# Row maxima of the first unit placed by transposes, and a shorter lead of the max products

## The chip, the cores and the metric

The kernel runs on one core of a Trainium2 chip. The metric is the device time of one execution in microseconds (us). The engines are TensorE (PE, with its weight loads PEld), VectorE (DVE), ScalarE (ACT), GpSimd (POOL) and SyncE (SP), which issues most of the DMA transfers.

## The reference

One block of a transformer with adaptive layer norms, on 2048 rows of 512 numbers in float32:

```python
mod = silu(c) @ w_mod                       # six rows of 512: sa, ca, ga, sb, cb, gb
h = layernorm(x) * (1 + ca) + sa
q = h @ wq                                  # 32 heads of 16
k = h @ wk; v = h @ wv                      # one head of keys and values, shared by all
p = softmax(q @ k.T * 16 ** -0.5)           # 2048 x 2048 for each head
x = x + ga * ((p @ v) @ wo)
h = layernorm(x) * (1 + cb) + sb
x = x + gb * (gelu(h @ w1 + b1) @ w2 + b2)  # 1376 hidden numbers
```

## The kernel before

**Precision.** A float32 number is kept as a high part, rounded to the format fp32r, and the remainder. A product of two such numbers is three products (`mm3`, and `batches` in the loop). The helper `split` makes the two parts; the engines that do it are its arguments.

**Units.** The 2048 rows are cut into 8 blocks of 256, the 32 heads into 8 groups of 4. A block and a group are one unit: 64 units. The queries of a unit lie in a tile `qst` of 128 partitions: its two halves `s` (partitions 0 to 63 and 64 to 127) hold two heads each. The keys lie in `ks` in the same two halves, for all 2048 keys. There are four `qst` tiles, used in turn (`QBUFS`), and `load_q` fills one with six transfers from HBM (eight from the fifth unit on).

**Two passes over the keys.** Softmax needs the largest score of each row. A first pass finds it: 32 *max products* `m` per unit (`Max.step`, L507), each with a reduction on VectorE (L512) that writes one column of `mx`. When the last one of a unit is done, `put_max` is called: VectorE reduces `mx` to 8 columns (L560) and transposes blocks of 32 x 32 (L561); `gather` puts the pieces into 8 rows on GpSimd (L555) and splits them into high part and remainder; `send` issues four transfers (L550) that write them into rows 48, 49, 112 and 113 of `qst`. In `ks` these rows are -1, so the second pass gets scores with the maximum subtracted: products `e` (`sexp`, L612), exponentials `p` on ScalarE (L616), and the products `acc` with the values and a block of ones (`pv`, L633), which sum up numerator and denominator. `finish_unit` copies them out.

**The loop** runs over the units and, in each, over 8 key steps of 256 keys, two at a time: a *pair*. A pair has 8 products `e`, 8 exponentials, 32 products `acc`, 8 max products of units that come later, and possibly one *batch* of weight products (query projections, output projection, the two layers of the network), cut in two halves of the array and mixed in. Weight products come from a queue of generators (`qproj_late`, `rest_steps`). In this loop the order on each engine is the order in which the program emits; it is not rearranged.

**The lead.** `lead[u]` says how many max products have been issued when unit u starts: all of units 0 to u and `4 * LEAD` more. It is 24 more here, so a unit's maxima are complete after the first pair of the unit before it. When no max products are left, the pairs run without them (`alone`).

**The clock.** `clock[0]` counts four ticks a pair. `later(n, fn)` runs `fn` n ticks on. In the loop `put_max` runs `reduce` at the next tick that is 1 above a multiple of four, `gather` `MAX_WAIT[0]` = 1 tick behind that and `send` `MAX_WAIT[1]` = 4 ticks behind it. Units 8 and 9 run `reduce` at once. The layer norm of the second half runs in the same clock: `stats`, `rstd` (L846, L847, L849), `xhat` (L852, GpSimd), `add_bias`, then transposes `tp` (L917, issued in batches).

**The prologue** makes layer norms, keys, values and the first query projections, and places the max products of the first units between them. `SLOTS` writes that order out: a number of max products, then named steps ("q 1": three products of the query projection of group 1, "rows": four vector-matrix products of `late_rows` (`modl`), "v 2": the values of block 2, "wq 2": a weight piece split on ScalarE and GpSimd, "load": `load_q` of unit 2). `FIRST_MAX` gives the order of the max products of units 0 and 1. In the prologue `later` runs its function at once. After the slots, `chunk(1)` goes on until `lead[0]`, 56 max products; `mod_state["rows"]` is copied by ScalarE (L1307, `modl_sb`), and `keep_warm(WARM[3])` issues five products whose result nobody reads (L287).

`ebank` gives out three PSUM banks in turn; the bank "x" holds in turn the key projection of block 3, the rows `modl` and late projections; max products have three banks "m" and in some pairs "x".

Of the kernel before, what the change touches and what calls it, by code (L numbers as in the profile page):

```python
# [8 lines left out]
F32 = mybir.dt.float32  # L9
F32R = mybir.dt.float32r  # L10
AF = mybir.ActivationFunctionType
ALU = mybir.AluOpType
AX = mybir.AxisListType

P = 128
# [3 lines left out]

GELU_R = 0.044715 ** 0.5  # L20

LEAD = 6
LEAD_0 = 6
FIRST_MAX = ((0, 0), (1, 0), (0, 1), (1, 1), (0, 2), (0, 3), (1, 2), (1, 3))
SLOTS = ((2, "keys 1", "keys 1"), (2, "keys 1", "keys 1"), (2, "low 1", "heads 2"), (2, "heads 2", "k 1"), (1, "warm"), (1, "heads 2"), (2, "heads 2", "v 0"),
# [4 lines left out]
MAX_WAIT = (1, 4)  # L30
QBUFS = 4
PREP = 4
BUSY = 5
# [3 lines left out]
TAIL = (4, 8)  # L37
GROUP = 4
NORM_WAIT = 6
WARM = (4, 16, 2, 5)  # L40
MOD_WAIT = 3
AHEAD = 4.5
STIR = ((0, 4, 8, 12), (16, 32, 48, 0))
# [2 lines left out]
def raw(ap):  # L46
    return ap.bitcast(F32)
# [3 lines left out]
def adaln_mqa_mlp(  # L51
# [15 lines left out]
    nc = tc.nc  # L67
    _, S, D = x.shape
# [4 lines left out]
    BQ = 512  # L73
# [4 lines left out]
    NKC = S // 512  # L78
# [28 lines left out]
    ident = const.tile([P, P], F32, name="ident")  # L107
# [16 lines left out]
    def ebank():  # L124
        turns[0] += 1
        return dict(tag=f"e{turns[0] % 3}", bufs=1)

    def split(dst_h, dst_l, src, eng_h, eng_l, between=None):
        if eng_h is nc.gpsimd:
            eng_h.tensor_scalar(out=dst_h, in0=src, scalar1=1.0, scalar2=0.0, op0=ALU.mult, op1=ALU.add)  # L130
        elif eng_h is nc.scalar:
            eng_h.copy(dst_h, src)
        else:
            eng_h.tensor_copy(out=dst_h, in_=src)
        if between:
            between()
        eng_l.tensor_tensor(out=dst_l, in0=src, in1=raw(dst_h), op=ALU.subtract)  # L137
# [7 lines left out]
    def later(n, fn):  # L145
        if draining[0]:
            fn()
        else:
            pending.append((clock[0] + n, fn))
# [7 lines left out]
    def mm3(ps, pairs, every=0, cost=0, begin=True, end=True):  # L157

        n, last = 0, 3 * len(pairs) - 1
        for wh, wl, xh, xl in pairs:  # L160
            for a, b_ in ((wh, xh), (wl, xh), (wh, xl)):
                nc.tensor.matmul(ps, a, b_, start=begin and n == 0, stop=end and n == last)  # L162
                n += 1
                if every and n % every == 0:
                    yield cost
# [48 lines left out]
    pro = pro_ctx.enter_context(tc.tile_pool(name="pro", bufs=1))  # L214
# [210 lines left out]
    def qpairs(b, g):  # L425
        hH, hL = hts[b]
        gs = slice(g * P, (g + 1) * P)
        return [(wqH[:, k, gs], wqL[:, k, gs], hH[:, k, :], hL[:, k, :]) for k in range(KD)]

    def qtiles(b, g):  # L430
        qH = att.tile([P, BQ], F32R, name=f"qH{b}_{g}", tag="xH", bufs=2)
        qL = att.tile([P, BQ], F32R, name=f"qL{b}_{g}", tag="xL", bufs=2)
        return qH, qL

    def qproj(b, g):

        ps = psum.tile([P, BQ], F32, name=f"qps{b}_{g}", tag="v" if g else "x")
        yield from mm3(ps, qpairs(b, g), 3, 1)
        qH, qL = qtiles(b, g)
        if g == 0:  # L440
            nc.scalar.copy(qH, ps)
            nc.vector.tensor_tensor(out=qL, in0=ps, in1=raw(qH), op=ALU.subtract)
        else:
            q32 = pro.tile([P, BQ], F32, name=f"q32_{b}_{g}", tag="h32", bufs=4)
            nc.scalar.copy(q32, ps)
            split(qH, qL, q32, act, pool)
        send_q(b, g, qH, qL)
        yield -2

# [16 lines left out]
    qsts = {}  # L466
# [15 lines left out]
    class Max:  # L482


        def __init__(self):
            def products(u, kcs):
                return [(u, j, t, kc) for kc in kcs for j in range(2) for t in range(blocks[units[u][0]][1] // P)]

            def in_rows(u):
                return [(u, j, t, kc) for j in range(2) for t in range(blocks[units[u][0]][1] // P) for kc in range(NKC)]  # L490


            begin = [o for u, kc in FIRST_MAX for o in products(u, [kc])]
            self.todo = [begin + [o for u in range(2, NU) for o in in_rows(u)] for _ in range(2)]
            self.mx, self.left, self.done = {}, list(size), 0

# [28 lines left out]
    placed = set()  # L525
# [5 lines left out]
    def put_max(u, mx):  # L531

        T = blocks[units[u][0]][1] // P
        qst = qsts[u]
        mm = mms[u % 2]
        turned = att.tile([P, 32], F32, name=f"turned{u}", tag="turned", bufs=2)
        if u == 0:
            pad(att, 256, "pad7")  # L540
        mt = att.tile([4 * T, P], F32, name=f"mt{u}", tag="mt", bufs=2)
        mh = att.tile([4 * T, P], F32R, name=f"mh{u}", tag="mh", bufs=2)
        ml = att.tile([4 * T, P], F32R, name=f"ml{u}", tag="ml", bufs=2)

        def send():
            for s in range(2):
                for r, src in ((48, mh), (49, ml)):
                    dst = qst[64 * s + r:64 * s + r + 1].rearrange("p j (t n) -> p (j t) n", n=P)
                    ring = nc.scalar if u == 0 and s else nc.sync
                    ring.dma_start(out=raw(dst), in_=raw(src[2 * T * s:2 * T * (s + 1), :].unsqueeze(1)))  # L550
            placed.add(u)

        def gather():
            for g in range(0, P, 32):
                nc.gpsimd.tensor_scalar(out=mt[:, g:g + 32], in0=turned[g:g + 4 * T, :], scalar1=1.0, scalar2=0.0,  # L555
                                        op0=ALU.mult, op1=ALU.add)
            split(mh, ml, mt, nc.gpsimd, nc.gpsimd)

        def reduce():
            nc.vector.tensor_reduce(out=mm[:, :4 * T], in_=mx, axis=AX.X, op=ALU.max)  # L560
            nc.vector.transpose(out=turned, in_=mm)  # L561
            later(MAX_WAIT[0], gather)
            later(MAX_WAIT[1], send)


        if NQ <= u < NQ + 2:
            reduce()
        else:
            later((0 - clock[0]) % 4 + 1, reduce)

    pbufs = {}
    ocs = []
# [606 lines left out]
    first = [sum(size[:u]) for u in range(NU + 1)]  # L1179
# [6 lines left out]
    act, dve, pool = nc.scalar, nc.vector, nc.gpsimd  # L1186
# [7 lines left out]
    projections = [qproj(b, g) for b in range(2) for g in range(KD)]  # L1194
# [36 lines left out]
    def q_group():  # L1231
        for i in range(KD):
            next(projections[0])
            if i == KD - 1:
                next(projections.pop(0))
            yield

    def warm():
        keep_warm(WARM[2], tag="x")
        yield  # L1240

    def one(fn, *args):
        fn(*args)
        yield
# [13 lines left out]
    turn1(0, 3)  # L1258
    keep_warm(WARM[0])
    mod1(0, 1, pool, dve, lambda: stats1(1))  # L1260
# [3 lines left out]
    rows = xhat1(1, act)  # L1264
# [17 lines left out]
    def last_h(t):  # L1282
        if t == QT - 1:
# [6 lines left out]
    run(xhat1(3, pool))  # L1290
    keep_warm(WARM[1])
    work = {"keys 1": keys(1), "heads 2": heads(2), "heads 3": heads(3), "q 1": q_group(), "keys 2": keys(2), "keys 3": keys(3),
            "v 0": one(v_out, 0), "v 1": one(v_out, 1), "v 2": one(v_out, 2), "v 3": one(v_out, 3), "rows": late_rows(),
            "low 1": one(low_k, 1), "low 2": one(low_k, 2), "low 3": one(low_k, 3), "k 1": one(repeat_k, 1), "k 2": one(repeat_k, 2), "k 3": one(repeat_k, 3), "load": one(load_q, 2), "warm": warm(),
            "wq 1": one(prep_wq, 1), "wq 2": one(prep_wq, 2), "wq 3": one(prep_wq, 3)}
    for n, *names in SLOTS:
        chunk(n)
# [173 lines left out]
    last = queue.pop()[1]  # L1471
# [49 lines left out]
```

## Time and profile before

| | |
|---|---|
| median of 3 runs | 1561.97 us (1561.87 to 1562.56) |
| profiled execution | 1561.89 us |
| its span, first to last instruction | 1560.1 us |
| prologue, until the first product `e` | 74.95 us |
| max products and their reductions | 2048, VectorE 1269.3 us busy |
| last max product's step ends | 1471.1 us |
| granted TensorE clock | 1.000 |

The profile is of one execution. "Busy" counts the time an engine works on instructions; matmuls overlap, so their durations are longer than their distances. The chain of waits is followed back from the last instruction: at each step to what released it, or to the instruction before it on its engine. In its rows the columns are start, duration, engine and line. In rows of the timeline they are start, duration, engine, line, operation, what is written and read, and in brackets the idle time before and what ended it.

### The profile page before, as it was taken

To read this page: it belongs to the slowest core of one execution; us is meant where nothing else is said; L and a number is where in the kernel's file an instruction comes from. 1 tells how busy PE (TensorE), PEld (TensorE's weight loads), DVE (VectorE), ACT (ScalarE), POOL (GpSimd) and SP (SyncE) were. 2 spreads that over 40 slices of the span, in tenths; PEclk is the share of its full clock that TensorE was granted. 3 is DMA by queue.
4 is the path that set the end of the run, shared out by engine and by line. 5 is a ranking of instruction groups with operands and counts; after the bars stand their busy time and mean duration, and the time that the engine had idled before them with its cause. 6 is when DMAs were issued, how large, how long until landed. Compare 5 with 4: busy or idle time off the path is not lost.

```text
span 1560.1 us, 41350 instructions
## 1 busy us (share of the span) xinstructions
PE 1543.2 (99%) x16347; PEld 955.2 (61%) x16347; DVE 1400.8 (90%) x2479; ACT 1227.4 (79%) x2392; POOL 681.5 (44%) x1194
## 2 busy tenths in 40 slices
PE   7999999999999999999999999999999999999999
PEld 4456555567655665557655675556655676556657
DVE  7999999999999999999999999999999999999725
ACT  5577778788878887788877887788877888778953
POOL 5545433867322570246522562245611474225721
PEclk9999999999999999999999999999999999999999
DMA  7225412312030211202012120302112120211241
GB/s 250 92 93 197 148 56 85 124 52 97 19 109 19 83 59 36 94 28 99 30 54 76 55 86 23 109 14 100 44 49 80 46 97 17 84 55 63 84 159 52
DMA packets 83125, 121.61 MB, mean 78 GB/s; under 512 B 19614, under 2 KB 56222, under 8 KB 82676
## 3 DMA queue, kind: packets, MB, share of 16 engines
q1 hardware_dynamic: 82916, 118.97, 22.9%
q8 instruction: 129, 2.11, 0.6%
q14 instruction: 64, 0.52, 0.1%
q10 hardware_dynamic: 16, 0.00, 0.0%
HBM read 91.13 MB, written 27.27 MB: 76 GB/s over the span
## 4 chain that ended last, share of the span: by engine, by line
PE 84%; DVE 10%; issue 3%; POOL 2%; DMA 1%; ACT 1%; SPq 0%; POOLq 0%; DVEq 0%
PE acc L633 28%; PE m L507 24%; PE e L612 15%; DVE mx L512 8%; PE w1ps L193 8%; PE w2ps L183 2%; PE w1ps L183 1%; DMA xt<-in_A_x_dram 1%; PE w2ps L193 1%; PE qps L193 1%; PE tp L193 1%; PE wops L193 1%; PE kps L162 1%; DVE st L840 1%; DVE x L833 1%
## 5 line engine op out<-in xcount | busy, mean ns | idle before, releaser
L512 DVE TENSOR_REDUCE mx<-m 128x1 f32<-128x512 f32 x2048 | 1269.3, 681 | 87.7 <-PE m L507 64.7
L616 ACT ACTIVATE p<-e 128x512 f32<-128x512 f32 x2048 | 1098.0, 598 | 254.8 <-PE e L612 106.4
L507 PE MATMUL m<-ks,qst 64*128 64x512 f32 x2048 | 832.9, 429 | 2.0 <-DVE mx L512 0.6
L612 PE MATMUL e<-qst,ks 64*128 64x512 f32 x2048 | 739.9, 413 | 0.0
L633 PE MATMUL acc<-p,va 128*32 128x256 f32 x8192 | 548.0, 385 | 0.0
L507 PEld LDWEIGHTS m<-ks,qst 64*128 64x128 f32 x2048 | 367.1, 184 | 211.6 <-DVE mx L512 174.0
L612 PEld LDWEIGHTS e<-qst,ks 64*128 64x128 f32 x2048 | 358.7, 185 | 92.3 <-ACT p L616 64.0
L633 PEld LDWEIGHTS acc<-p,va 128*32 128x32 f32 x8192 | 214.5, 109 | 213.7 <-issue 110.7
L555 POOL TENSOR_SCALAR mt<-turned 8x32 f32<-8x32 f32 x256 | 53.1, 208 | 419.5 <-DVE turned L561 407.4
L193 PE MATMUL w1ps<-h2H,w1t 64*128 64x256 f32 x1216 | 232.7, 287 | 0.0
L193 PEld LDWEIGHTS w1ps<-h2H,w1t 64*128 64x128 f32 x1216 | 183.6, 185 | 28.4 <-issue 14.4
L193 PE MATMUL w1ps<-h2L,w1t 64*128 64x256 f32 x608 | 167.0, 275 | 0.0
L193 PE MATMUL w2ps<-w2H,gH 64*128 64x512 f32 x264 | 115.9, 439 | 0.0
L193 PEld LDWEIGHTS w1ps<-h2L,w1t 64*128 64x128 f32 x608 | 112.8, 185 | 0.0
L193 PE MATMUL w2ps<-w2L,gH 64*128 64x512 f32 x264 | 103.4, 392 | 0.0
L193 PE MATMUL w2ps<-w2H,gL 64*128 64x512 f32 x264 | 103.0, 390 | 0.0
L959 POOL TENSOR_SCALAR tt<-tt 128x256 f32<-128x256 f32 x77 | 31.0, 403 | 143.1 <-ACT tt L958 109.8
L137 POOL TENSOR_TENSOR gL<-z,gH 128x256 fp32r<-128x256 f32 x77 | 56.9, 739 | 6.4
L960 POOL TENSOR_TENSOR tt<-tt,z 128x256 f32<-128x256 f32 x77 | 56.8, 738 | 6.4
L970 POOL TENSOR_TENSOR z<-tt,z 128x256 f32<-128x256 f32 x77 | 56.4, 733 | 6.0
L969 POOL TENSOR_TENSOR tt<-tt,z 128x256 f32<-128x256 f32 x77 | 56.5, 734 | 0.0
L193 PE MATMUL wops<-woH,onH 64*128 64x512 f32 x112 | 49.8, 444 | 0.0
(190 smaller groups left out, 1495.3 us busy)
## 6 DMA issues: line engine op xcount, KB each, us to landing
w1t<-dw SPq DMA_DIRECT2D x82, 512.0 KB
qst<-dq SPq DMA_DIRECT2D x384, 32.0 KB
do<-oc SPq DMA_DIRECT2D x64, 128.0 KB
dw<-w1s SPq DMA_DIRECT2D x11, 512.0 KB
xt<-in_A_x_dram SPq DMA_DIRECT2D x4, 1024.0 KB
dq<-qH SPq DMA_DIRECT2D x16, 256.0 KB
dq<-qL SPq DMA_DIRECT2D x16, 256.0 KB
x<-in_A_x_dram SPq DMA_DIRECT2D x8, 512.0 KB
```

Of the source, the lines that this page charges most:

```text
L137: eng_l.tensor_tensor(out=dst_l, in0=src, in1=raw(dst_h), op=ALU.subtract)
L183: nc.tensor.matmul(ps, a, b_, start=first_, stop=last_)
L193: ins = nc.tensor.matmul(ps, a[rows], b_[rows], start=first_ and s == 0, stop=last_ and s == 1)
L507: nc.tensor.matmul(m, qsts[u][rows, j, t * P:(t + 1) * P], ks[rows, kc * 512:(kc + 1) * 512], start=True, stop=True)
L512: nc.vector.tensor_reduce(out=self.mx[u][:, i, kc:kc + 1], in_=m, axis=AX.X, op=ALU.max)
L555: nc.gpsimd.tensor_scalar(out=mt[:, g:g + 32], in0=turned[g:g + 4 * T, :], scalar1=1.0, scalar2=0.0, op0=ALU.mult, op1=ALU.add)
L612: nc.tensor.matmul(e, ks[rows, kt * P:(kt + 1) * P], rhs, start=True, stop=True)
L616: ins = nc.scalar.activation(dst, e, AF.Exp, scale=0.25)
L633: ins = nc.tensor.matmul(accs[u][32 * cidx:32 * cidx + 32, :], va[:, kt, :], rhs, start=kt == 0, stop=kt == NKT - 1)
L960: nc.gpsimd.tensor_tensor(out=tt, in0=tt, in1=z, op=ALU.mult)
L969: nc.gpsimd.tensor_tensor(out=tt, in0=tt, in1=z, op=ALU.mult)
L970: nc.gpsimd.tensor_tensor(out=z, in0=tt, in1=z, op=ALU.add)
```

## The change

Three things change together.

*The first unit's rows.* For unit 0 `put_max` no longer transposes, gathers and sends. VectorE reduces to 8 columns as before, copies them into column 48 (and, for the second half, 112) of four zeroed 128 x 128 tiles `spots`, and writes the remainder into column 49 (113). A new step, `first_rows`, transposes the four tiles on TensorE into one PSUM bank and adds that bank to the whole `qst` on VectorE. Its rows are thus placed without a transfer. `spots` is cleared by GpSimd in a step of its own.

*The order.* Unit 0's max products are complete after 46 products instead of 48, because one group of unit 1's moves behind them. `LEAD` goes from 6 to 4: the lead is 16 products, the loop starts after 48 instead of 56, and a unit's maxima are complete after the second pair of the unit before it. The slots are rewritten; the query projection's last step becomes a fifth slot, with the remainder on GpSimd and the two transfers there. The five keep-warm products go.

*The waits.* For later units `gather` is called right behind `reduce`, and `send` 2 ticks behind it.

```diff
-LEAD = 6
-LEAD_0 = 6
-FIRST_MAX = ((0, 0), (1, 0), (0, 1), (1, 1), (0, 2), (0, 3), (1, 2), (1, 3))
+LEAD = 4
+LEAD_0 = 4
+FIRST_MAX = ((0, 0, 4), (1, 0, 4), (0, 1, 4), (1, 1, 3), (0, 2, 4), (0, 3, 4), (1, 1, 1), (1, 2, 4), (1, 3, 4))
...
-         (0, "v 2"), (2, "q 1"), (2, "q 1"), (2, "q 1"),
-         (2, "q 1", "rows"), (2, "v 3", "wq 2"), (2, "rows"), (2, "rows"), (2, "rows", "wq 3", "load"))
-MAX_WAIT = (1, 4)
+         (0, "v 2", "q 1", "spots"), (2, "rows"), (2, "q 1"), (2, "q 1", "wq 2"), (2, "q 1"), (2, "q 1", "rows"),
+         (2, "first", "rows", "v 3", "rows", "wq 3", "load"))
+MAX_WAIT = 2
...
-WARM = (4, 16, 2, 5)
+WARM = (4, 16, 2, 0)
...
-            split(qH, qL, q32, act, pool)
+            nc.scalar.copy(qH, q32)
+            yield -2
+            nc.gpsimd.tensor_tensor(out=qL, in0=q32, in1=raw(qH), op=ALU.subtract)
...
+        if u == 0:
+            nc.vector.tensor_reduce(out=mm[:, :4 * T], in_=mx, axis=AX.X, op=ALU.max)
+            src = mm[:, :4 * T].rearrange("p (s n) -> p s n", s=2)
+            dst = spots.rearrange("p n (s c) -> p s n c", s=2)
+            nc.vector.tensor_copy(out=dst[:, :, :, 48], in_=src)
+            nc.vector.tensor_tensor(out=dst[:, :, :, 49], in0=src, in1=raw(dst[:, :, :, 48]), op=ALU.subtract)
+            return
...
-                    ring = nc.scalar if u == 0 and s else nc.sync
-                    ring.dma_start(out=raw(dst), in_=raw(src[2 * T * s:2 * T * (s + 1), :].unsqueeze(1)))
+                    nc.sync.dma_start(out=raw(dst), in_=raw(src[2 * T * s:2 * T * (s + 1), :].unsqueeze(1)))
...
-            later(MAX_WAIT[0], gather)
-            later(MAX_WAIT[1], send)
+            gather()
+            later(MAX_WAIT, send)
...
+    spots = pro.tile([P, 4, P], F32R, name="spots")
+
+    def clear():
+        nc.gpsimd.memset(raw(spots), 0.0)
+
+    def first_rows():
+
+        qst = qsts[0].rearrange("p j n -> p (j n)")
+        ps = psum.tile([P, BQ], F32, name="rows0", **ebank())
+        for n in range(4):
+            nc.tensor.transpose(ps[:, n * P:(n + 1) * P], raw(spots[:, n, :]), ident)
+        nc.vector.tensor_tensor(out=qst, in0=ps, in1=raw(qst), op=ALU.add)
+        placed.add(0)
```

The lines left out are the lists that give the maxima's order one product at a time, the generator of the query projection with its fifth step, the 256-byte padding tile that is now made with unit 1, and the two new names in the table of steps.

More of the change, by code (lines that the diff above doesn't have):

```diff
@@ L490, in in_rows @@
                 return [(u, j, t, kc) for j in range(2) for t in range(blocks[units[u][0]][1] // P) for kc in range(NKC)]
-            begin = [o for u, kc in FIRST_MAX for o in products(u, [kc])]
+            parts = {(u, kc): products(u, [kc]) for u in range(2) for kc in range(NKC)}
+            begin = [parts[u, kc].pop(0) for u, kc, n in FIRST_MAX for _ in range(n)]
+            assert not any(parts.values())
             self.todo = [begin + [o for u in range(2, NU) for o in in_rows(u)] for _ in range(2)]
@@ L537, in put_max @@
         mm = mms[u % 2]
+        if u == 0:
[5 more added lines that the diff above has]
+            return
         turned = att.tile([P, 32], F32, name=f"turned{u}", tag="turned", bufs=2)
-        if u == 0:
+        if u == 1:
             pad(att, 256, "pad7")
@@ L1234, in q_group @@
             if i == KD - 1:
-                next(projections.pop(0))
+                last = projections.pop(0)
+                next(last)
             yield
+        next(last, None)
+        yield
     def warm():
@@ L1293, in adaln_mqa_mlp @@
             "v 0": one(v_out, 0), "v 1": one(v_out, 1), "v 2": one(v_out, 2), "v 3": one(v_out, 3), "rows": late_rows(),
-            "low 1": one(low_k, 1), "low 2": one(low_k, 2), "low 3": one(low_k, 3), "k 1": one(repeat_k, 1), "k 2": one(repeat_k, 2), "k 3": one(repeat_k, 3), "load": one(load_q, 2), "warm": warm(),
+            "low 1": one(low_k, 1), "low 2": one(low_k, 2), "low 3": one(low_k, 3), "k 1": one(repeat_k, 1), "k 2": one(repeat_k, 2), "k 3": one(repeat_k, 3), "load": one(load_q, 2), "warm": warm(), "first": one(first_rows), "spots": one(clear),
             "wq 1": one(prep_wq, 1), "wq 2": one(prep_wq, 2), "wq 3": one(prep_wq, 3)}
```

## The prediction

> **What bounds the kernel now.** I read the page first, then the chain of waits around the first unit, in the steady loop and at its end, then single engines in the windows that the chain names.
>
> ```profile
> PE 1543.2 (99%) x16347; PEld 955.2 (61%) x16347; DVE 1400.8 (90%) x2479; ACT 1227.4 (79%) x2392; POOL 681.5 (44%) x1194
> ...
> PE 84%; DVE 10%; issue 3%; POOL 2%; DMA 1%; ACT 1%; SPq 0%; POOLq 0%; DVEq 0%
> ```
>
> TensorE (PE) is the bound, with VectorE (DVE) close behind: 84% and 10% of the chain. So I price an instruction by whether PE or DVE runs without a pause where it stands. Every key step (K step) ends in 16 products `acc` of 1.00 us, so the distance of these rows is the price of a step. The chain at the end of the loop:
>
> ```profile
> 1468.33 1.00 PE acc L633 x16
> ...
> 1471.17 1.00 PE acc L633 x16
> ...
> 1476.36 1.00 PE acc L633 x16
> ```
>
> With max products a step takes 2.84 us, a pair of steps 5.68. From 1471.17 the max products are used up, and a pair takes 5.19.
>
> The start of the loop, in the same view:
>
> ```profile
> 64.52 0.90 PE qps L162 x3
> 65.42 1.00 PE modl L292 x8
> 66.42 0.43 PE m L507 x2
> ...
> 73.66 0.33 PE idle L287
> 73.99 1.12 issue
> 75.10 0.59 ACT modl_sb L1307
> ```
>
> Here the bound isn't the rows of maxima alone: ScalarE (ACT) copies `modl_sb` at 75.10, when the five keep-warm products have just ended, and every exponential is queued behind that copy. It ends at 75.69.
>
> **The start, step by step.** Up to the value projection of block 2 both kernels issue the same on PE; it starts at 58.42:
>
> ```profile
> 58.42 0.43 PE L414 MATMUL vps<-ident,vt 32*128 32x32 f32 x4
> ```
>
> From there PE runs, in the new order: `vps` (0.36 until the next row), the first q group's three products (0.90), two max products (0.43): 60.1. Now `rows` needs the bank "x", which frees when VectorE has subtracted block 3's keys:
>
> ```profile
> 59.90 0.68 DVE L402 TENSOR_TENSOR ks<-kps,ks 16x512 fp32r<-16x512 f32 x1
> ```
>
> That is 60.6. Then `rows` 1.0, three times max pair and q group (3 x 1.33), the pair that completes unit 0: it starts at 65.6.
>
> ```profile
> 66.89 2.48 DVE L512 TENSOR_REDUCE mx<-m 128x1 f32<-128x512 f32 x4 [1.05 <-PE m L507]
> 69.40 0.19 DVE L560 TENSOR_REDUCE mm<-mx 128x8 f32<-128x32 f32 x1
> ```
>
> A pair's reductions start 0.47 after it (66.42 to 66.89) and take 1.24 (half of 2.48): 67.3. VectorE's three small steps (maxima of maxima, copy into `spots`, remainder) follow. Only the first has a row, 0.19. The other two, 8 numbers a partition, lie between that and the 0.68 of a 512-wide operation; I take 0.2 each, as the row of that size says: 67.9. Meanwhile PE has done the next `rows` and max pair by 67.5 and waits half a microsecond. Behind the waiting transposes stand two `rows`, a `vps` and the loop's first products. The four transposes cost what four of the same size do:
>
> ```profile
> 37.18 0.59 PE tp L375 x4
> ```
>
> They end at 68.6; two `rows` and a `vps` (2.36) end at 70.9. The wide addition on VectorE (0.68, behind two reductions) is done by 70.1 and hidden under them; without that cover it would cost its 0.68. The copy `modl_sb` has no keep-warm products to wait for, and ends 0.6 later: 71.5, with 0.2 for semaphores 71.7. Against 75.69 the loop starts **3.9 us** earlier. With 0.68 for both small steps it is 3.0; with no semaphore cost 4.1. What goes away besides (gather, four row transfers, eight max products) was beside this path or is in it already. What moves with it: the q group's two transfers and `load_q`'s six wait one slot longer, but unit 2's first max product comes 16 products into the loop, two pairs or 11.4 us; GpSimd clears `spots` in a slot in which nothing else is queued on it, ten max products ahead of the first use.
>
> The five keep-warm products go and transposes come, so the clock is to be looked at. This stretch now:
>
> ```profile
> 58.40:75.00 16.60, 15.99 (x81) 6.72 (x79) 14.92 (x26) 5.03 (x12) 5.59 (x12) 1.00 0.10 35
> ```
>
> The granted clock is 1.00, with a pause of 1.12 us in it. I expect it to stay, since the new pauses are of half a microsecond. The Trainium skill, "TensorE: Matmul & The Clock Gate", speaks against this part: PE's clock halves after an idle window of about 3.4 us, and transposes don't count as busy (Part 1 and Part 4). By its window two pauses of half a microsecond cost nothing, by its transposes the margin shrinks; the trace agrees so far that short pauses leave the clock alone. A clock that falls is the last rival.
>
> **The end: one pair more with max products.** The lead shrinks by 8 products, one pair's worth, so the max products last one pair longer. That pair costs 5.68 in place of 5.19: **+0.5**.
>
> **The middle: the reductions move by one pair.** Each later unit's maxima are complete one pair later, so its small reduction and transpose on VectorE move from the unit's second pair to its third. (The program counts four ticks a pair.) In steps that PE bounds this costs nothing: four reductions take 2.35 (the row below has four) of 2.84, and a pair leaves twice the rest, about 1.0, for 0.5. But once per block, seven times,
>
> ```profile
> POOL ve L847 <- DVE mv L846: 27.1, 7, 4.5
> ```
>
> the third pair has no weight products, and VectorE bounds it, loaded with the layer norm's statistics. The chain there:
>
> ```profile
> 852.26 0.24 DVE mv L846 x2
> 852.51 2.35 DVE mx L512 x4
> 854.87 0.04 issue
> 854.91 0.50 PE m L507
> ```
>
> VectorE runs without a pause, and PE's max product at 854.91 waits for it. What is put in front of 852.26 delays it in full. The price, and what the old place gives back:
>
> ```profile
> 845.70 0.17 DVE L560 TENSOR_REDUCE mm<-mx 128x8 f32<-128x32 f32 x1
> 845.98 0.21 DVE L561 STREAM_TRANSPOSE turned<-mm 128x32 f32<-128x32 f32 x1
> ```
>
> ```profile
> 845.60 0.49 PE L507 MATMUL m<-ks,qst 64*128 64x512 f32 x1
> ```
>
> The two take 0.38 us of work and 0.49 from start to end, I use 0.46. At the old place VectorE would only wait for this product, which ends at 846.09, as long as for the two: almost nothing comes back. 7 x 0.46 = **+3.2**. The lower end is zero, if the next steps take it up.
>
> GpSimd (POOL) has the same collision, because the gather now comes at once, in front of `ve` and the two `xh`:
>
> ```profile
> 846.28 1.02 POOL L555 TENSOR_SCALAR mt<-turned 8x32 f32<-8x32 f32 x4 [20.87 <-DVE turned L561]
> 847.38 0.29 POOL L130 TENSOR_SCALAR mh<-mt 8x128 fp32r<-8x128 f32 x1
> 847.75 0.46 POOL L137 TENSOR_TENSOR ml<-mt,mh 8x128 fp32r<-8x128 f32 x1
> 852.60 0.24 POOL L847 TENSOR_SCALAR ve<-mv 128x2 f32<-128x2 f32 x1 [4.39 <-DVE mv L846]
> 852.92 0.72 POOL L849 TENSOR_TENSOR rs<-ve,mhalf 128x2 f32<-128x2 f32 x1
> 853.75 4.15 POOL L852 TENSOR_SCALAR xh<-x,mv,rs 128x512 f32<-128x512 f32 x2
> ```
>
> The gather and split take 1.93 (846.28 to 848.21) and would end near 854.7, so `ve` starts 2.1 later and the second `xh` ends at 860.0 in place of 857.9. The first weight load that needs it:
>
> ```profile
> 859.62 0.30 PEld L193 LDWEIGHTS tp<-ident,xh 64*128 64x128 f32 x2
> ```
>
> It is itself late by the 0.46, 860.08: covered, by almost nothing. Without VectorE's delay, PE would wait 0.4 here instead; the two overlap and don't add.
>
> The rows' four transfers move from the fourth tick after the reduction to the second:
>
> ```profile
> 849.74 0.57 SPq L550 DMA_DIRECT2D qst<-ml  x1
> ```
>
> ```profile
> 858.95 0.29 PEld L612 LDWEIGHTS e<-qst,ks 64*128 64x128 f32 x2
> ```
>
> The next unit's first product is at 858.95, 13.2 after the reduction at 845.70; one pair less leaves 7.6. The last transfer is issued by 850.31, 4.6 after the reduction. No row shows its landing apart. Unit 0 has the whole way, its transfers shared by two queues:
>
> ```profile
> 74.95 0.49 PE L612 MATMUL e<-qst,ks 64*128 64x512 f32 x2
> ```
>
> From 69.40 that is at most 5.6; two more issues on the one queue (0.6 each) make 6.8, which fits into 7.6.
>
> **Sum.** -3.9 + 0.5 + 3.2 = -0.2 us. The profiled execution took 1561.89 (span 1560.1 and 1.8 around it); the median of the runs is 1561.97, so both stand for the same. Forecast **1561.7**. Its own bounds: -3.0 to -4.1 at the start, so 1561.5 to 1562.6.
>
> **Rivals.**
> *VectorE's half microsecond is taken up* (PE runs ahead on its banks, or the old place gives it back after all, since the chain of waits passes through the small reduction there too): -3.9 + 0.5 = -3.4, 1558.5. Against it: the wait at 854.91, which nothing in between can shorten.
> *The rows come late* (slower). Mechanism: at some unit starts the four transfers stand behind other issues of SyncE (SP), and PE's first product of the unit waits. It decides from 0.8 us of delay (7.6 less 6.8). One block's four issues
>
> ```profile
> 805.05 2.47 SPq L767 DMA_DIRECT2D os<-drs  x4
> ```
>
> in front would be 1.7 too late, in seven blocks 12 us: 1573.5. Against it: by the program these are issued at tick 8 of their unit, and the moved reduction comes at tick 9, so they are mostly gone when its rows are ready.
> *The change does not start the loop as early as it says*: PE's wait for the transposes grows, because the small steps cost more or wait for each other. With 2.0 for the start: 1563.6.
> *The clock*: at half speed the loop's first pair costs its 5.68 again: 1567.4.
>
> **How the numbers follow.** Forecast 0.53; VectorE's share free 0.27; rows late 0.09; start less 0.08; clock 0.03. 0.2% is 3.1 us, about what a measurement of this kernel can tell from no change. The forecast and the weak start lie within it (0.61), the free share 3.4 below is faster (0.27), late rows and clock are slower (0.12). The range takes in the free share with the start's upper bound and, above, the weak start with 1.4 for small losses elsewhere: 1558.3 to 1565.0; only late rows and clock, 0.12, are left out.
>
> **What would show it.** Right: first exponential 3 to 4 us earlier; `modl_sb` directly behind `modl`; transposes about half a microsecond after the max pair in front of them; the steps after each layer norm's statistics longer by about 0.45 in seven places; six pairs without max products at the end in place of seven. Wrong: those seven places unchanged (then 1558.5), PE waiting at a unit's first `e` product, or a granted clock under 1.00 after the start.

## The result

The changed kernel takes 1571.38 us (median of 6 runs, 1570.41 to 1572.46) against 1562.2 for the kernel before (6 runs beside them): a ratio of 1.0055, 95% interval 1.0042 to 1.0068. It is slower by 9.2 us, where 1561.7 was forecast. The profiled execution took 1571.4 (span 1569.6, before 1560.1). The row of the products `e` in the page of the profile, after and then before:

```profile
L636 PE MATMUL e<-qst,ks 64*128 64x512 f32 x2048 | 742.9, 412 | 4.3 <-DMA qst<-ml 4.2
```

```profile
L612 PE MATMUL e<-qst,ks 64*128 64x512 f32 x2048 | 739.9, 413 | 0.0
```

The busy times say nothing: each engine does as much as before (TensorE 1545.6 us after 1543.2, VectorE 1402.1 after 1400.8). This row does. It is a group of 2048 products; behind the second bar stands the idle time ahead of them and what ended most of it. In the whole kernel they wait 4.3 us, where they waited 0.0 before, and 4.2 of these for one thing, the rows of maxima (`qst<-ml`).

The distances of the `acc` rows from step to step, before and after, place the difference. All numbers are of the two profiled executions:

| where | after less before, us | forecast |
|---|---|---|
| up to the value projection of block 2 (`vps`, 58.42 and 59.07) | +0.65 | 0 |
| from there to the first exponential (17.16 and 15.28) | -1.88 | -3.9 |
| unit 12's start, one step | +5.91 | 0 |
| seven steps behind a layer norm's statistics | +2.4 | +3.2 |
| the two steps of the added pair at the end | +0.5 | +0.5 |
| seven other steps (+0.43 to -0.20) | +1.1 | 0 |
| behind the last `acc` (0.6 of it one transfer, 4.00 in place of 3.42) | +0.7 | 0 |

These add up to 9.4 of the span's 9.5. The first line is no effect of the change: `vps` starts between 57.8 and 59.1 in the executions below, which all give TensorE the same work up to there. The first loads of some take longer than those of others; that is a part of it, and the rest was not traced. So the start is counted from `vps` in all that follows.

**The start.** The timeline of the changed kernel; the columns are start, duration, engine, and in brackets the idle time ahead and its releaser:

```profile
65.07 0.72 ACT L337 CAST wqH<-wqf 128x256 fp32r<-128x256 f32 x2 [2.97 <-PE qps L162]
65.56 1.43 POOL L338 TENSOR_TENSOR wqL<-wqf,wqH 128x256 fp32r<-128x256 f32 x2 [7.10 <-ACT wqH L337]
...
65.84 0.50 PE L162 MATMUL qps<-h0H,wqH 128*128 128x512 f32 x1 [0.39 <-ACT wqH L337]
...
67.05 0.51 PE L162 MATMUL qps<-h0H,wqL 128*128 128x512 f32 x1 [0.70 <-POOL wqL L338]
...
69.18 1.27 POOL L448 TENSOR_TENSOR qL<-q,qH 128x512 fp32r<-128x512 f32 x1 [2.19 <-ACT qH L446]
...
69.56 0.19 DVE L543 TENSOR_REDUCE mm<-mx 128x8 f32<-128x32 f32 x1
69.85 0.64 DVE L546 CAST spots<-mm 128x8 fp32r<-128x8 f32 x1
...
70.52 0.17 DVE L547 TENSOR_TENSOR spots<-mm,spots 128x8 fp32r<-128x8 f32 x1
...
70.75 0.66 PE L591 MATMUL rows<-ident,spots 128*128 128x128 f32 x4 [1.12 <-DVE spots L547]
...
73.87 0.59 ACT L1334 COPY modl_sb<-modl 128x512 f32<-128x512 f32 x1 [0.21 <-issue]
74.35 4.03 ACT L640 ACTIVATE p<-e 128x512 f32<-128x512 f32 x8
```

The end of the chain is as forecast: no keep-warm products in front of `modl_sb`, transposes of 0.66. Two things were not. The fourth product of the q group waits for a cast and a remainder of `wq` (0.39 and 0.70): the new order puts "wq 2" between the group's third and fourth step. It prepares another quarter of the tile than the product reads, and yet the product waits. And VectorE's copy of 8 numbers a partition (the row CAST) takes 0.64 where I had taken 0.2; the remainder behind it, of the same size, takes 0.17.

**Unit 12.** The timeline there:

```profile
332.82 0.18 DVE L570 TENSOR_REDUCE mm<-mx 128x8 f32<-128x32 f32 x1
...
333.58 1.29 POOL L1161 TENSOR_TENSOR w2f<-w2f,gb 128x512 f32<-128x512 f32 x1
...
340.25 1.02 POOL L565 TENSOR_SCALAR mt<-turned 8x32 f32<-8x32 f32 x4
...
345.49 0.76 PE L636 MATMUL e<-qst,ks 64*128 64x512 f32 x1 [4.19 <-DMA qst<-ml]
```

VectorE has the maxima at 332.8, but GpSimd gathers them only at 340.25, because two pieces of `w2` (three operations and 3.3 us each, the first from 333.58) stand in front. From there all goes as fast as anywhere; the first product of the unit stands for 4.2. In the kernel before, one pair was the whole distance between the gather and such a piece:

```profile
328.26 1.02 POOL L555 TENSOR_SCALAR mt<-turned 8x32 f32<-8x32 f32 x4
...
333.83 1.28 POOL L1137 TENSOR_TENSOR w2f<-w2f,gb 128x512 f32<-128x512 f32 x1
```

What follows the wait is slow too. The window (busy time and count of PE, PEld, DVE, ACT, POOL; granted clock; DMA share; GB/s):

```profile
344.00:348.00 4.00, 2.51 (x17) 2.54 (x18) 1.06 (x2) 1.20 (x2) 0.00 (x0) 0.64 0.11 27
```

The clock is at 0.64 of full speed over these 4 us; from 345.49 to the next `acc` at 348.56 pass 3.07, where the same stretch took 1.51 before (341.23 to 342.74).

**A layer norm's statistics**, the place quoted in the prediction, VectorE's rows before and now:

```profile
851.85 0.41 DVE L840 BATCH_NORM_STATS2 st<-x 128x6 f32<-128x256 f32 x1
852.18 0.33 DVE L846 BATCH_NORM_AGGREGATE mv<-st 128x2 f32<-128x12 f32 x2
852.42 9.00 DVE L512 TENSOR_REDUCE mx<-m 128x1 f32<-128x512 f32 x15
```

```profile
858.55 0.42 DVE L864 BATCH_NORM_STATS2 st<-x 128x6 f32<-128x256 f32 x1
858.88 0.17 DVE L570 TENSOR_REDUCE mm<-mx 128x8 f32<-128x32 f32 x1
859.16 0.21 DVE L571 STREAM_TRANSPOSE turned<-mm 128x32 f32<-128x32 f32 x1
859.29 0.24 DVE L870 BATCH_NORM_AGGREGATE mv<-st 128x2 f32<-128x12 f32 x2
859.45 4.82 DVE L516 TENSOR_REDUCE mx<-m 128x1 f32<-128x512 f32 x8
```

The two small steps stand where the forecast put them. From the start of `st` to that of `mx` pass 0.90; before it were 0.57. They cost 0.33 and not 0.46, because `mv` needed 0.33 before and needs 0.24 now. My reading, which no run tests, is that it had waited for `st`, and that the small steps fill that wait.

### The profile page after: what moved, and what is told of

Same layout as the page of the kernel before. It is cut to its first block, busy times and chain, and to the rows that moved or that the text cites. A ratio compares the mean times of both kernels' runs of the same rounds, so it can differ in the third digit from the quotient of the medians.

```text
span 1569.6 us, 41361 instructions
## 1 busy us (share of the span) xinstructions
PE 1545.6 (98%) x16358; PEld 954.7 (61%) x16358; DVE 1402.1 (89%) x2481; ACT 1228.5 (78%) x2392; POOL 680.2 (43%) x1189
## 4 chain that ended last, share of the span: by engine, by line
PE 92%; DVE 5%; DMA 1%; ACT 1%; POOL 0%; issue 0%; SPq 0%; DVEq 0%; ACTq 0%
PE acc L657 31%; PE m L511 27%; PE e L636 17%; PE w1ps L193 8%; DVE mx L516 4%; PE w2ps L183 2%; PE wops L193 1%; PE qps L193 1%; PE w1ps L183 1%; PE w2ps L193 1%; PE tp L193 1%; PE kps L162 1%; PE modr L292 0%; PE tp L375 0%; DMA wm<-in_w_mod_dram 0%
## 5 line engine op out<-in xcount | busy, mean ns | idle before, releaser
L193 PE MATMUL w1ps<-h2H,w1t 64*128 64x256 f32 x1232 | 237.0, 288 | 0.0
```

Of the source, the lines that this page charges most:

```text
L193: ins = nc.tensor.matmul(ps, a[rows], b_[rows], start=first_ and s == 0, stop=last_ and s == 1)
```

## The experiments

Each ratio is to the kernel before, run beside it. The theory: three mechanisms that the sum has (start, end, seven places), and on top of them collisions that it lacks: the wq piece, VectorE's copy, and GpSimd's queue at unit 12 with the clock behind it. The main rival: the lead of 16 itself, or the new rows themselves, cost the time.

### e1: the wq piece behind the q group

```diff
-         ... (2, "rows"), (2, "q 1"), (2, "q 1", "wq 2"), (2, "q 1"), (2, "q 1", "rows"),
+         ... (2, "rows"), (2, "q 1"), (2, "q 1"), (2, "q 1"), (2, "q 1", "rows", "wq 2"),
```

> The changed kernel, with one edit: the preparation of the third quarter of wq (ScalarE cast and GpSimd remainder, 'wq 2') stands behind the q group of block 1, where it stood between the group's third and fourth step. Theory: in the changed kernel TensorE waited 0.39 and 0.70 us for this cast and this remainder, although the fourth q product reads another quarter; with both gone the first exponential comes 1.1 us earlier and the time falls by 1.1, from 1571.4 to 1570.3. Rival: the wait was hidden, because the maxima's small steps on VectorE and the copy of the modulation rows on ScalarE set the start, or because the moved cast now delays that copy: time unchanged at 1571.4, first exponential as before.

Measured 1570.7, ratio 1.0057 (1.0044 to 1.0070): no difference from the changed kernel that can be told. The start, though, is 0.87 shorter (14.41 from `vps` to the first exponential). VectorE's rows show why not 1.1:

```profile
66.53 1.27 POOL L448 TENSOR_TENSOR qL<-q,qH 128x512 fp32r<-128x512 f32 x1 [9.31 <-ACT qH L446]
66.90 0.19 DVE L543 TENSOR_REDUCE mm<-mx 128x8 f32<-128x32 f32 x1
67.19 0.64 DVE L546 CAST spots<-mm 128x8 fp32r<-128x8 f32 x1
67.75 1.43 POOL L338 TENSOR_TENSOR wqL<-wqf,wqH 128x256 fp32r<-128x256 f32 x2
67.86 0.65 DVE L547 TENSOR_TENSOR spots<-mm,spots 128x8 fp32r<-128x8 f32 x1
```

The remainder, 0.17 before, now takes 0.65, and what is new is the GpSimd piece beside it. The copy ends when `qL` ends (67.8). In e4 below the copy starts later, only 0.33 before `qL` ends, and takes 0.36 (69.61 to 69.97, `qL` to 69.94), so what it takes is set by `qL`. The reduction in between, while `qL` runs, takes its usual 0.19. And 0.96 of what the start won was lost at unit 12, where the wait was as long (4.22) but the clock stayed low longer: the `acc` group behind it took 1.93 in place of 1.07.

### e2: unit 12's gather in front of the w2 pieces

```diff
+        state["due"] = u
 ...
             gather()
+            state["due"] = 0
 ...
-            ... weights[0] in preps and not state["busy"]:
+            ... weights[0] in preps and not state["busy"] and state.get("due") != 12:
```

> The changed kernel, with one edit: where unit 12's rows of maxima are due, the two w2 pieces on GpSimd are put behind the gather of these rows, where they stood in front of it; no other order changes on any engine. Theory: the two pieces (6.7 us of GpSimd) are what makes the rows late; TensorE's wait of 4.2 us at unit 12 and the stretch at half clock behind it (1.3) go, and the time falls by 5.5 to 6, to 1565.4 to 1565.9. Rival one: the rows are late for another reason, such as the issue of their transfers one pair after the reduction: the wait stays, 1571.4. Rival two: only the wait goes and the slow products come from something else: 1567.2.

Measured 1565.12, ratio 1.0019 (1.0010 to 1.0028): 6.3 less, and the step at unit 12 is 5.92 shorter than in the changed kernel. GpSimd there:

```profile
333.63 1.02 POOL L565 TENSOR_SCALAR mt<-turned 8x32 f32<-8x32 f32 x4
...
335.52 1.28 POOL L1163 TENSOR_TENSOR w2f<-w2f,gb 128x512 f32<-128x512 f32 x1
```

VectorE's transpose starts at 333.15, so the gather follows within 0.5. Only GpSimd's order differs, so this cause is shown. The rows need no longer lead; they need a free GpSimd.

### e3: the later units' lead back at 24

```diff
-LEAD = 4
+LEAD = 6
```

> The changed kernel with the lead of the later units back at 24 products and that of the loop's start kept at 16: the new rows of the first unit, the new order of the prologue and the gather at once stay. Theory: the lead is what costs, the rows don't: unit 12's wait, the seven places at the layer norm's statistics (0.33 each) and the pair at the end (0.5) go, 5.9 + 2.3 + 0.5 = 8.7 less, so between 1560.3 (the kernel before less the 1.9 us that the new start gains from the value projection of block 2 on) and 1562.7 (the changed kernel less 8.7). Rival one: the cost comes with the gather at once or with the new start, not with the lead: about 1571. Rival two: only unit 12 hangs on the lead and the seven places on the gather: 1565.5.

Measured 1566.1, ratio 1.0022 (1.0013 to 1.0031): a miss. Step by step against the changed kernel, unit 12 (-5.92), the seven places (-0.2 to -0.6 each) and the end (-0.22 and -0.27) went as the theory says. But the eight products that the lead needs are made up in the first block, in pairs of ten in place of eight, and four such pairs cost 0.9 to 1.2 each; with smaller ones it comes to some 4.6. I had not counted that.

### e4: products of no use in unit 12's wait

```diff
+            if (u, K) == (12, 0):
+                ps = psum.tile([P, BQ], F32, name="spare", tag="m", bufs=3)
+                for i in range(17):
+                    nc.tensor.matmul(ps, ks[:, 0:P], ks[:, 0:BQ], start=True, stop=True)
```

> The changed kernel with 17 products of no use (4.1 us at 0.243 each) put in front of unit 12's first step, where TensorE waits 4.2 us for the rows. Theory: the products behind the wait run at half speed because TensorE stood still for over 4 us; with the stretch filled the granted clock there stays at 1.00 in place of 0.64, the products come every 0.115 in place of 0.213, and the time falls by 1.2 to 1570.2, while the rows are as late as before. Rival: the slow products come from something else, such as the transfers and the other engines that start together behind the wait: nothing changes, 1571.4, or it rises by what the filled stretch takes beyond the wait.

Measured 1569.73, ratio 1.0045 (1.0033 to 1.0058); the step at unit 12 is 1.25 shorter than in the changed kernel, as expected to 0.05.

```profile
344.00:348.00 4.00, 3.79 (x43) 2.46 (x43) 2.58 (x4) 2.34 (x5) 0.00 (x0) 1.00 0.16 34
```

```profile
340.13 4.15 PE L1388 MATMUL spare<-ks 128*128 128x512 f32 x17
...
344.91 0.47 PE L636 MATMUL e<-qst,ks 64*128 64x512 f32 x1 [0.21 <-DMA qst<-ml]
```

With the pause filled the clock stays at 1.00. So of the 5.9 at unit 12, some 1.25 are the clock that falls while TensorE stands still; the rest is the wait. This is the rule that the prediction cited against the change (the Trainium skill, "TensorE: Matmul & The Clock Gate", Part 1: the clock halves after an idle window of about 3.4 us); the trace agrees with it, at a pause of 4.2 and at another place than I had weighed.

### e5 and e6: the copy as a reduction; all collisions together

e5 is e1 with

```diff
-            nc.vector.tensor_copy(out=dst[:, :, :, 48], in_=src)
+            nc.vector.tensor_reduce(out=dst[:, :, :, 48], in_=mx.rearrange("p (s n) k -> p s n k", s=2), axis=AX.X, op=ALU.max)
```

> Base: the run with the wq piece behind the q group (1570.7). One edit: VectorE's copy of the first unit's maxima into the cleared tile (0.64 us there) is a second small reduction straight into it. Theory: the copy and the remainder behind it take 0.64 in place of 0.17 because each runs until the GpSimd piece beside it ends (a remainder of q, then one of wq): a reduction isn't held, so the second one takes 0.19, but the remainder behind it is now held by the q remainder and ends between 0.0 and 0.65 earlier than in the base, the transposes with it: 1570.0 to 1570.7. Rival: a copy into this tile simply takes 0.64 (strided 8 numbers a partition): then the reduction into it takes as long, nothing changes, and the remainder behind it is as long as before whatever runs on GpSimd.

Measured 1569.85, ratio 1.0047 (1.0033 to 1.0060), and a start of 13.75 (0.66 less than e1). e6 has this and e2's edit, and "wq 2" ahead of the q group:

```diff
-         (2, "low 2", "k 2", "v 1", "wq 1"), ...
+         (2, "low 2", "k 2", "v 1", "wq 1", "wq 2"), ...
```

> The changed kernel with three edits: the preparation of the third quarter of wq stands right behind that of the second, ahead of the q group, so that no piece of it runs beside VectorE's small steps or in front of a q product; the copy into the cleared tile is a small reduction; the two w2 pieces stand behind unit 12's gather. Theory: the terms add: 1565.1 (the run with only the third edit) less 0.9 (the wait for the wq piece) less 0.65 (one held step on VectorE) makes 1563.6, with the transposes directly behind the end of the q remainder on GpSimd; still slower than before by about 1, which is the 7 places and the pair at the end. Rival: the start is bound elsewhere (the modulation rows, ScalarE's copies, the maxima) and nothing is won by the first two: 1565.1; or the earlier cast delays block 3's keys on ScalarE: over 1565.1.

Measured 1562.29, ratio 1.0005 (0.9996 to 1.0014): level with the kernel before, 1.3 better than expected. Start 13.73, which is the gain that was expected there. What goes beyond it is mostly one step in the profiles: at unit 10 e2's first product had waited 0.66 for its rows and its step took 3.74; in e6 it takes 2.85. I come back to that wait at e9. VectorE in e6:

```profile
67.36 1.28 POOL L448 TENSOR_TENSOR qL<-q,qH 128x512 fp32r<-128x512 f32 x1 [7.90 <-ACT qH L446]
...
67.85 0.18 DVE L546 TENSOR_REDUCE spots<-mx 128x8 fp32r<-128x32 f32 x1
68.06 0.61 DVE L547 TENSOR_TENSOR spots<-mm,spots 128x8 fp32r<-128x8 f32 x1
```

The reduction into the same strided places takes 0.18, so the 0.64 is not the price of the layout. The remainder is held again, until `qL` ends at 68.64.

### e7: a lead of 20

e7 is e6 without e2's edit, and

```diff
-LEAD = 4
+LEAD = 5
```

> As the run before, with a lead of 20 products for the later units in place of the two w2 pieces' move. By the program each later unit's small reduction then falls half a pair before the pair of the layer norm's statistics. Theory: the seven places (0.33 each, 2.3) and half of the end's 0.5 go; four more max products in the first block cost 0.5 each on VectorE (eight cost 4.1 in the run with lead 24): 1563.6 less 2.5 plus 2.1, about 1563.2, so no gain worth the name. Rival: the four products fit into the first block where VectorE has room: 1561.1.

Measured 1572.92, ratio 1.0069 (1.0056 to 1.0083): a miss. My reading of the program was wrong. Half of each unit's products belong to either half of the array and are issued in either half of a pair, so with four products more lead the last one still falls into the same half pair, and the small reductions and the gather of unit 12 stay where they are (340.99 here, behind two `w2` pieces). Unit 12 costs its 5.8 again, and the four products cost some 3.4 in the first block. It says the same as e2 once more, from the other side, and nothing new on the seven places.

### e8: the small steps twice

```diff
-            nc.vector.tensor_reduce(out=mm[:, :4 * T], in_=mx, axis=AX.X, op=ALU.max)
-            nc.vector.transpose(out=turned, in_=mm)
+            for _ in range(2 if u > 1 else 1):
+                nc.vector.tensor_reduce(out=mm[:, :4 * T], in_=mx, axis=AX.X, op=ALU.max)
+                nc.vector.transpose(out=turned, in_=mm)
```

on top of e2.

> The run with the two w2 pieces behind unit 12's gather (1565.1), in which VectorE makes each later unit's small reduction and transpose twice (0.38 us more, 62 times). Theory: this costs only where VectorE bounds the pair, at the seven places behind the layer norm's statistics, 0.33 to 0.46 each, and nothing in the other units: 2.3 to 3.2 more, 1567.4 to 1568.3. Rival one: VectorE's small steps cost at every unit: 62 x 0.38 = 23.6 more, 1588.7. Rival two: what costs at the seven places is GpSimd's gather in front of the layer norm's steps, not VectorE: nothing more, 1565.1.

Measured 1584.48, ratio 1.0142 (1.0128 to 1.0156): 19.4 more than e2. The theory falls, and for a second set of small steps rival one is nearly right: 0.31 a unit for 0.38 of work. At six of the seven places it is 0.44 to 0.57, but an ordinary unit costs 0.2 to 0.47 too. One such step, in the kernel before (where the small steps stand in another pair), in e2 (one set) and in e8 (two sets):

```profile
761.05 2.48 DVE L512 TENSOR_REDUCE mx<-m 128x1 f32<-128x512 f32 x4 [0.22 <-PE e L612]
```

```profile
760.29 1.07 PE L659 MATMUL acc<-p,va 128*32 128x256 f32 x16
...
761.87 2.44 DVE L516 TENSOR_REDUCE mx<-m 128x1 f32<-128x512 f32 x4
...
762.57 0.50 PE L511 MATMUL m<-ks,qst 64*128 64x512 f32 x1
763.00 1.07 PE L659 MATMUL acc<-p,va 128*32 128x256 f32 x16
```

```profile
768.41 1.07 PE L660 MATMUL acc<-p,va 128*32 128x256 f32 x16
...
769.64 0.17 DVE L571 TENSOR_REDUCE mm<-mx 128x8 f32<-128x32 f32 x1
769.85 0.21 DVE L572 STREAM_TRANSPOSE turned<-mm 128x32 f32<-128x32 f32 x1
...
770.45 2.44 DVE L516 TENSOR_REDUCE mx<-m 128x1 f32<-128x512 f32 x4
...
771.15 0.49 PE L511 MATMUL m<-ks,qst 64*128 64x512 f32 x1
771.57 1.07 PE L660 MATMUL acc<-p,va 128*32 128x256 f32 x16
```

With no small steps the step takes 2.70 (`acc` at 759.52 and 762.22 in the kernel before), with one set 2.71, with two 3.16. VectorE's four reductions start 1.53, 1.58 and 2.04 after the `acc` ahead of them. So the first set costs nothing that can be told: most of it falls into VectorE's rest (0.22 in the first row), and it delays the four by 0.05. The second set, 0.38 of work, adds 0.45. In e2 and e8 the last max product of the step comes 0.70 after the start of the four reductions; by the program it needs the bank that the first of them empties. So what stands directly in front of these four is on TensorE's path as soon as it no longer fits into VectorE's rest of that one step, however much rest there is over the whole pair.

### e9 and e12: the last held step, and GpSimd at unit 10

e9 is e6 with the q group's last step behind the transposes:

```diff
-         ... (2, "rows"), (2, "q 1"), (2, "q 1"), (2, "q 1"), (2, "q 1", "rows"),
-         (2, "first", "rows", "v 3", "rows", "wq 3", "load"))
+         ... (2, "rows"), (2, "q 1"), (2, "q 1"), (2, "rows"), (2, "q 1"),
+         (2, "first", "rows", "q 1", "v 3", "rows", "wq 3", "load"))
```

> The run with the three edits (1562.3) and one more: the last step of the q group of block 1 stands behind the first unit's transposes in place of two max pairs ahead of them, so that GpSimd's remainder of q (1.28) no longer runs beside VectorE's remainder of the maxima. Theory: that VectorE step (0.61) was held by GpSimd's and takes 0.17 now; the transposes come 0.45 earlier and the time falls to 1561.8; VectorE's row has the 0.17. Rival: the step takes 0.6 for itself in this place, or the q products behind the transposes now delay the loop by what the transposes win: 1562.3 or more.

Measured 1562.54, ratio 1.0002 (0.9993 to 1.0011): no gain. But the step is free as the theory says, and the start is 13.39:

```profile
67.87 0.17 DVE L547 TENSOR_TENSOR spots<-mm,spots 128x8 fp32r<-128x8 f32 x1
...
68.50 1.30 POOL L448 TENSOR_TENSOR qL<-q,qH 128x512 fp32r<-128x512 f32 x1 [9.35 <-ACT qH L446]
...
295.09 0.47 PE L638 MATMUL e<-qst,ks 64*128 64x512 f32 x1 [1.04 <-DMA qst<-ml]
```

The last row tells where it went in the profiled execution: unit 10's rows, gathered behind `w2` pieces like unit 12's, were 1.04 late, and that step 1.28 longer than in e6. But that execution took 1563.74, the longest of the eleven, 1.2 above their median. And the wait at unit 10 comes and goes from execution to execution: 0.07 in the changed kernel and 0.66 in e2, which run the same program up to there, 0.41 in e1, 0.28 in e5, none in e4 and e6. So the profile doesn't show what became of the start's 0.34 in the other ten. e12 keeps a piece out of that place too:

```diff
-            ... state.get("due") != 12:
+            ... state.get("due") not in (10, 12):
```

> The run before (1562.5) with one more edit: a w2 piece is also kept out of the way of unit 10's gather on GpSimd (it comes one pair later). In that run the start was 0.6 earlier than in the one it was built on, but unit 10's first product waited 1.04 for its rows, which GpSimd had gathered behind two w2 pieces, and the step there was 1.28 longer. Theory: what the start wins is given back where GpSimd, which doesn't start earlier, ends the wait; with the piece out of the way the 1.28 comes back: 1561.2, the kernel before less 1.0, which leaves 3.8 at the start less 2.3 at the seven places and 0.5 at the end. Rival: the lost time was not the rows: 1562.5.

Measured 1562.08, ratio 0.9998 (0.9989 to 1.0007). The 1.28 came back in the profile, as the theory says. The median moved by 0.5, and the intervals of e9 and e12 overlap, so a gain of the theory's size isn't shown; against the kernel before there is no difference. From the first `acc` on, this version is 3.72 ahead of the kernel before, and 0.33 ahead at the last one: the lead of 16 gives the rest back.

### e11: the new rows with the old lead

e11 is e9 without e2's edit, and

```diff
-LEAD = 4
-LEAD_0 = 4
+LEAD = 6
+LEAD_0 = 6
```

> The same with the lead of 24 products back from the start on (eight more max products ahead of the loop, none more in the first block) and the two w2 pieces where they were: the new rows alone, without the smaller lead. Theory: the seven places, the pair at the end and unit 12's wait are as in the kernel before, since the small reductions fall where they fell there; at the start eight products cost between 2.0 (TensorE, 0.25 each) and 5.0 (VectorE, 0.62 each) of the 3.4 to 3.9 that the new start wins. So 1562.1 (before) less 3.9 plus 2.0 to 5.0: 1560.2 to 1563.2. Rival: the rows were never what held the start, and the gain at the start is the eight products alone: then it comes out at 1562.1 plus the 0.5 to 1 of the transposes, 1562.6 to 1563.1.

Measured 1565.31, ratio 1.0021 (1.0012 to 1.0030): above both. No wait at unit 12 and no loss at the seven places, but the first exponential comes 17.65 after `vps`, later than in the kernel before (17.16):

```profile
72.19 9.69 DVE L516 TENSOR_REDUCE mx<-m 128x1 f32<-128x512 f32 x16 [1.80 <-PE m L511]
...
76.58 3.56 ACT L640 ACTIVATE p<-e 128x512 f32<-128x512 f32 x7 [4.16 <-PE e L636]
```

The eight products stand in a row ahead of the loop, VectorE needs 9.69 for 16 reductions, and the first `e` waits behind them. The window there:

```profile
76.00:78.00 2.00, 2.00 (x10) 1.39 (x7) 2.00 (x4) 1.42 (x3) 0.00 (x0) 0.50 0.06 18
```

The clock falls on top of it, to 0.50. So without the eight products less, the new way of the rows wins nothing at the start. Whether the eight products less would win as much with the old way of the rows, no run tests; and the clock is mixed into this one.

## Why the prediction was wrong

Of the 9.7 us between forecast and result, 5.9 are unit 12 and 2.0 the start; the rest is small terms of either sign.

**The start, -3.9: mis-sized, the mechanism right.** It was -1.88. The missing 2.0 are, by the runs, 0.87 for the wait on the wq piece (e1), 0.66 to 0.68 for the copy and one held step (e5, e6) and 0.34 for the last held step (e9, whose start, unlike its time, shows it). With all three out, the start is 13.38 against 17.16, which is -3.78. The rival of a weak start had this size (2.0), and half of the reason: it named the small steps, not the piece of `wq`. The failed sentences are two. "From there PE runs" counted the steps that the diff moves, but not "wq 2", which it moves as well. "I take 0.2 each" was right for the remainder when GpSimd is free (0.17); the copy stood beside `qL` in every run that has it, and took 0.36 to 0.65. The rule for this stands in the Trainium skill, "SBUF — State Buffer" (Who interferes with whom): VectorE and GpSimd share a pair of ports as an exclusive lock; a copy in a mode that uses both port pairs, or an operation with two inputs in SBUF beside a GpSimd operation that reads SBUF, waits for a GpSimd operation that started first, and a reduction doesn't. The rows agree: the copy 0.64, the remainder 0.61 to 0.65 beside GpSimd and 0.17 without it, reductions 0.18 to 0.19 in either case. Which mode the copy ran in, no trace shows.

**The end, +0.5: right** (0.22 and 0.28).

**The seven places, +3.2: right in place and kind, too large.** 2.4 measured, 0.33 in most, since `mv` had a wait of its own. That the old place gives nothing back held: the step there is as long as before (2.84). In the other units "in steps that PE bounds this costs nothing" held too, for the one set that moves: a step is as long with it as without it (2.70 and 2.71 in the rows of e8). The reason given was too generous, though. "A pair leaves twice the rest, about 1.0, for 0.5" counts both steps of the pair; e8 shows that only the rest of the one step counts, and that it holds one set and not two.

**The rows late: the rival that came true, by another engine.** The step that failed is "7.6 less 6.8". Its 6.8 came from unit 0 and a layer norm's pair, where GpSimd gathers within 0.3 of the transpose. I priced the rival by SyncE's queue and looked at GpSimd only there; at unit 12, 6.7 of `w2` pieces stood in the way, and the row of the piece at 333.83 in the profile of before, 5.6 behind the gather, would have said so. One unit in place of seven, but 5.9 in all: 4.2 of wait and some 1.25 to 1.7 for the clock behind it.

**The clock: right at the start of this execution** (1.00 from 58.5 to 75.5), but with some luck: e4 and e8 have the same start, and there the clock fell to 0.50 for 3.4 us, and the start was 15.62 and 15.64 in place of 15.28. And it was wrong to weigh the clock there only.

**The sum.** With the collisions removed (e6, e12) the kernel is where the sum put it, level with the kernel before: in e12 -3.7 at the start, +0.5 at the end, +2.6 at the seven places, +0.3 of small change up to the last `acc` and +0.5 behind it. None of these versions beats the kernel before by more than can be told.

## What to carry to other kernels

Ahead of a moved step, list what stands in every queue that it passes at every instance of the loop, not at the one that was looked at: the preparations of weights in the background come in a few units only, and one such place was worth more than all the rest of the change. A margin taken from one place holds for that place; the tightest one decides. And a small VectorE step in this loop, which TensorE bounds, was free while it fitted into VectorE's rest in front of the reductions that TensorE waits for, and nearly all of what went beyond it was paid; VectorE's share of busy time over the pair doesn't tell which (e8).

## What the hardware showed

- A VectorE remainder of 0.17 took 0.61 to 0.65 when a GpSimd operation with two inputs had started before it, and ended with it (e1, e5, e6; 0.17 in e9, where none ran). The copy took 0.36 to 0.65 and always ended within 0.04 of it. Reductions took 0.18 to 0.19 in the same place.
- The clock fell to 0.50 without a long pause, too: in e11 TensorE gave one max product every 0.60 from 72.94 to 75.33, and the clock stayed at 0.50 from 75.3 until about 82.1. In e4 and e8 it fell at 66.5 and 66.9 for 3.4 us behind waits of 0.39 and 0.70, which the changed kernel has in the same place at a clock of 1.00; why there and not here stays open.
- The slow stretch that goes with the same pause of 4.2 differs in place and length. In the changed kernel the clock is at 0.50 from 345.1 to 348.6, which begins at the end of the pause (341.3 to 345.5); in e1 from 342.0 to 348.9, which begins in its middle (339.5 to 343.7) and takes the `acc` group behind it too. Every slow stretch between the start and the end of these profiles lasts 3.4 us or twice that.
